# VectorE's share of the softmax exponentials: eight steps a tile against five, four of them over two tiles

## The chip, the cores and the metric

The kernel runs on one core of a Trainium2 chip. The time is the device time of one launch in microseconds; of several runs the median counts. The engines are TensorE (PE in the profile, its weight loads PEld), VectorE (DVE), ScalarE (ACT), GpSimd (POOL) and SyncE (SP), which here only issues DMAs.

## What is computed

Two layers over 2048 tokens of width 448. Each layer is an attention block with 16 heads of 28 columns, followed by a mixing block with two small square matrices and an MLP of width 1792. The part that matters here is attention:

```python
q, k, v = qkv[0], qkv[1], qkv[2]
scores = jnp.einsum("bhqd,bhkd->bhqk", q, k) * (Dh ** -0.5)
p = _softmax(scores, axis=-1)
o = jnp.einsum("bhqk,bhkd->bhqd", p, v)
...
x = x + _A_ref(_layernorm(x, axis=-1), A_wqkv, A_wo)
x = x + _B_ref(_layernorm(x, axis=-1), B_w1, B_w2, B_w3, B_w4)
x = x + _A_ref(_layernorm(x, axis=-1), A_wqkv, A_wo)
x = x + _B_ref(_layernorm(x, axis=-1), B_w1, B_w2, B_w3, B_w4)
```

A layer has 16 heads x 2048 x 2048 exponentials; as tiles of 128 keys by 512 queries that is 1024 tiles, 2048 for both layers. The softmax needs no maximum over the row: every query's scores are shifted by a bound that is written into a spare row of the queries (WSH is a part of it), and a column of ones beside the values gives the sum, by which the result is divided later.

## The kernel before

**Who fixes the order.** The program is not written engine by engine. Small tasks (Python generators) yield operations with an engine, an assumed duration, what they read and write, and a rank; class `Sched` (lines 185 to 539) plays them against assumed durations and puts each engine's instructions in one fixed order; class `Plan` then adds the semaphore waits. On the chip each engine goes through its list in order. Large tables steer this: `RANK` (line 562), the lead at which queries are projected (`Q_LEAD`), which engine does a shared step (`XPAR`, keys 'ez', 'ex', 'ek', 'eo', 'eq': 0 GpSimd, 1 VectorE, 2 whichever is free), and the rates below. Where TensorE would be idle, `keep_pe_busy` puts in filler matmuls (line 2267).

**The stream of score tiles.** Work goes by segments: a chunk of queries, a group of four heads, a range of keys. There are 68 segments with 512 key blocks in all, four tiles (one a head) to a key block. `t_scores` (line 1629) cuts the stream of tiles into units of two or three: even units use PSUM banks 0 to 2, odd units 3 and 4 (and 5 if it is free). The scores come from line 1487; `t_exp` (line 1740) has ScalarE take a whole unit in one instruction (line 1754) into PT. `t_pv` (line 1768) multiplies the exponentials with the values (line 831, four heads side by side) and adds up in bank 7, two key blocks at a time, in the order of the stream.

**Tiles for VectorE.** `ahead_of` (line 1640) picks a tile some key blocks ahead of the stream, so that VectorE has time for it. There are two kinds. A ring tile takes the third bank of an even unit, so that ScalarE's instruction is two tiles wide; it is chosen 6 to 8 blocks ahead (RLO, RHI), if VectorE's planned load over the last 3 us is below XPAR 'dt' and the segment's count is within `R_RATE`. A side tile takes a bank of its own beside the unit, 5 to 7 blocks ahead (DLO, DHI), if the share of fillers over the last 8 us is above XPAR 'ft' and the count is within `D_RATE`. Either needs a y buffer (two in yd, two more in idle parts of vaug at some times) and a PD slot (four, one more in vaug), held until line 831 has used the tile.

**The eight steps.** `d_first` (line 1582) reads the scores from PSUM and writes them as int16 in units of 1/256 of a power of two; `d_chain` (line 1595) turns that into a bf16 value by seven steps over 512 elements: shift out the fraction (line 1611), two factors of a polynomial (1613, 1615, 1617), their product (1619), the sum (1621), and a shift back with the exponent's offset (1624). One of three fb buffers is held from line 1611 to 1621; fb also serves the softmax's division (line 1861) and the tanh form of gelu (line 2034).

Other lines that the prediction names: 1257 (squares of the keys), 1509 (shift of the queries at a new key range).

Of the kernel before, what the change touches and what calls it, by code (L numbers as in the profile page):

```python
# [184 lines left out]
class Sched:  # L185
# [43 lines left out]
    def _advance(self, t):  # L229
        while True:  # L230
# [29 lines left out]
            elif c == "rel":  # L260
# [3 lines left out]
                self.res_t[spec[1]] = max(self.res_t.get(spec[1], 0.0), self.clock)  # L264
            elif c == "reserve":
                if spec[2]:
                    self.reserved.add(spec[1])
                else:
                    self.reserved.discard(spec[1])
            elif c == "wait":  # L270
                if spec[1] not in self.events:
                    self.waiters.setdefault(spec[1], []).append(t)
                    return
            elif c in ("acq", "ready"):
                self.pendq.append(t)
                return
            else:
                self.opq.append(t)
                return
# [270 lines left out]
DST = [0.2, 0.2, 0.336, 0.2, 0.336, 0.336, 0.2]  # L550
DSEG = 1
R_RATE = {(0,): 0, (1,): 0.006, (2,): 0.016, (3,): 0.04, (4,): 0.006, (5,): 0.051, (6,): 0.059, (7,): 0, (8,): 0.06, (9,): 0.048, (10,): 0.024, (11,): 0.15, (12,): 0.066, (13,): 0.022, (14,): 0.022, (15,): 0.192, (16,): 0.233, (17,): 0.075, (18,): 0.115, (19,): 0.273, (20,): 0.093, (21,): 0.233, (22,): 0.355, (23,): 0.29, (24,): 0, (25,): 0.268, (26,): 0.146, (27,): 0.207, (28,): 0.183, (29,): 0.243, (30,): 0.071, (31,): 0.163, (32,): 0.241, (33,): 0.078}
# [9 lines left out]
RANK = {('q', 0, 1): 2.187, ('q', 0, 2): 1.163, ('q', 0, 3): 2.532, ('q', 1, 0): 1.046, ('q', 1, 1): 2.224, ('q', 1, 2): 2.603, ('q', 1, 3): 1.838, ('b', 0, 0): 2.161, ('b', 0, 1): 2.168, ('b', 0, 2): 1.786, ('b', 0, 3): 3, ('b', 0, 4): 1.341, ('b', 1, 0): 2.813, ('b', 1, 1): 2.272, ('b', 1, 2): 2.447, ('b', 1, 3): 2.996, ('b', 1, 4): 1.2, ('a', 0, 0): 1.465, ('a', 0, 1): 1.069, ('a', 0, 2): 2.708, ('a', 0, 3): 1.394, ('a', 0, 4): 2.037, ('a', 1, 0): 2.44, ('a', 1, 1): 2.73, ('a', 1, 2): 1.987, ('a', 1, 3): 2.129, ('a', 1, 4): 2.296, ('k', 0, 1): 2.195, ('k', 0, 2): 2.331, ('k', 0, 3): 1.257, ('k', 1, 0): 2.95, ('k', 1, 1): 2.469, ('k', 1, 2): 2.057, ('k', 1, 3): 1.894, ('k', 1, 4): 1.325, ('c', 0, 0): 2.53, ('c', 0, 1): 1.416, ('c', 0, 2): 2.652, ('c', 0, 3): 2.702, ('c', 0, 4): 2.848, ('c', 1, 0): 1.131, ('c', 1, 1): 1.73, ('c', 1, 2): 1.159, ('c', 1, 3): 1, ('c', 1, 4): 2.718, ('w', 0, 0): 3, ('w', 0, 1): 2.526, ('w', 0, 2): 2.67, ('w', 0, 3): 2.558, ('w', 0, 4): 1.161, ('w', 1, 0): 1.012, ('w', 1, 1): 2.213, ('w', 1, 2): 2.397, ('w', 1, 3): 1.705, ('w', 1, 4): 1.73, ('o', 0, 0): 2.913, ('o', 0, 1): 2.031, ('o', 0, 2): 2.592, ('o', 0, 3): 1.459, ('o', 0, 4): 2.576, ('o', 1, 0): 1.548, ('o', 1, 1): 1.29, ('o', 1, 2): 2.296, ('o', 1, 3): 1, ('o', 1, 4): 2.51, ('v', 0, 1): 1, ('v', 0, 2): 2.093, ('v', 0, 3): 2.749, ('v', 1, 0): 2.464, ('v', 1, 1): 1.304, ('v', 1, 2): 1.601, ('v', 1, 3): 1, ('v', 1, 4): 2.552, ('l', 1, 0): 2.0, ('l', 1, 1): 1.613, ('l', 1, 2): 2.72, ('l', 1, 3): 2.152, ('l', 1, 4): 1.196}  # L562
Q_LEAD = {(0, 1): 7, (0, 2): 102, (0, 3): 50, (1, 0): 86, (1, 1): 54, (1, 2): 9, (1, 3): 71}
# [29 lines left out]
def QLEAD(L, qc):  # L593
    return Q_LEAD[L, qc]

# [5 lines left out]
def build_kernel(nc, A_x, A_wqkv, A_wo, B_x, B_w1, B_w2, B_w3, B_w4, out, n_layers=2):  # L601
# [22 lines left out]
    NPD = 4  # L624
# [1746 lines left out]
```

## Time and profile before

| | |
|---|---|
| median of 3 runs | 1026.12 us (1024.83 to 1026.28) |
| span of the profiled execution, first to last instruction | 1023.9 us |
| busy, share of the span: PE, ACT, DVE, POOL | 95%, 95%, 82%, 21% |
| granted TensorE clock | 1.000 |
| line 1754, first and last start | 15.2 and 968.7 us |

The profile gives the span of the profiled execution; its own device time is not recorded beside it, so the median of the runs stands for it, 2.2 us above the span. In the rows, "us, mean ns" after the bar are the busy time of a group and the mean duration of one instruction, and what follows the second bar is the idle time of that engine before them and what ended it. Rows by stretches give busy microseconds and, in brackets, the number of instructions for each engine in turn, then the granted clock, the DMA engines' share and GB/s.

### The profile page before, as it was taken

The page shows a single profiled execution, that of the slowest core. Times are in us where ns is not written, and L with a number is a line of the kernel's source. Part 1 is how long each engine was busy: PE and PEld are TensorE (multiplying, and loading weights), DVE is VectorE, ACT ScalarE, POOL GpSimd, SP SyncE. Part 2 cuts the span into 40 slices and gives each one's busy share as a digit, 9 for nine tenths or more (in the row PEclk, how much of TensorE's full clock was granted, in tenths as well). Part 3 has the DMA queues.
Part 4 walks back from the last instruction along what each step waited for, and adds up shares of the span by engine and source line. Part 5 has one row for each costly group of instructions (what it writes and reads, how often), then busy time and mean ns, then how long its engine had stood idle before and what let it go on. Part 6 is the DMA issues. An engine that isn't in the chain of part 4 may idle for free.

```text
span 1023.9 us, 36349 instructions
## 1 busy us (share of the span) xinstructions
PE 973.4 (95%) x16102; PEld 404.7 (40%) x16102; DVE 843.5 (82%) x2134; ACT 973.6 (95%) x897; POOL 220.1 (21%) x350
## 2 busy tenths in 40 slices
PE   8999899999999999999999999999999999999998
PEld 4333344334343334344344333333333333444465
DVE  8879999988768778897788888997898888788752
ACT  6899999999999999999999999999999999999942
POOL 4003022143213013350212010112332200331220
PEclk9999999999999999999999999999999999999999
DMA  4534228121203113321133024324311110220000
GB/s 126 130 74 140 59 76 216 34 44 37 33 18 84 43 49 88 51 39 19 36 87 63 22 76 140 112 80 112 74 29 33 32 55 13 55 61 17 13 21 25
DMA packets 98829, 64.43 MB, mean 63 GB/s; under 512 B 70832, under 2 KB 87552, under 8 KB 98672
## 3 DMA queue, kind: packets, MB, share of 16 engines
q1 hardware_dynamic: 94176, 53.11, 21.1%
q0 software_dynamic: 3376, 8.09, 3.0%
q8 instruction: 126, 2.06, 0.9%
q10 hardware_dynamic: 1120, 0.92, 0.3%
q14 instruction: 31, 0.25, 0.1%
HBM read 28.16 MB, written 16.76 MB: 44 GB/s over the span
## 4 chain that ended last, share of the span: by engine, by line
ACT 62%; PE 23%; DVE 12%; DMA 1%; issue 1%; ACTq 0%; SPq 0%; DVEq 0%
ACT PT L1754 55%; PE ps L840 12%; PE ps L1487 5%; PE ps L831 4%; ACT h2T L2220 3%; PE ps L2267 1%; ACT fb L2036 1%; DVE yd L1584 1%; DMA xT<-xnd 1%; DVE fb L1619 1%; DVE fb L1615 1%; DVE PD L1624 1%; DVE ub L1840 1%; DVE vaug L1621 1%; ACT L1754 1%
## 5 line engine op out<-in xcount | busy, mean ns | idle before, releaser
L1754 ACT ACTIVATE PT<-ps 128x1024 bf16<-128x1024 f32 (+1 forms) x791 | 877.8, 1288 | 7.8 <-PE ps L1487 6.6
L1487 PE MATMUL ps<-qT,kT 32*128 32x512 bf16 (+1 forms) x2560 | 310.1, 340 | 23.5 <-ACT PT L1754 17.7
L831 PE MATMUL ps<-PT,vaug 128*32 128x512 bf16 (+1 forms) x2396 | 243.8, 341 | 0.5 <-ACT PT L1754 0.3
L1487 PEld LDWEIGHTS ps<-qT,kT 32*128 32x128 bf16 x2560 | 79.7, 91 | 292.0 <-ACT PT L1754 262.9
L840 PE MATMUL ps<-xT,w 128*32 128x512 bf16 (+3 forms) x2592 | 178.7, 343 | 1.7 <-issue 0.8
L2267 PE MATMUL ps<-ident 128*32 128x256 bf16 x2508 | 123.0, 280 | 2.2 <-POOL ident L930 1.5
L831 PEld LDWEIGHTS ps<-PT,vaug 128*32 128x32 bf16 x2396 | 71.8, 94 | 91.5 <-issue 78.2
L840 PE MATMUL ps<-w,h2T 128*32 128x448 bf16 x1288 | 89.5, 355 | 2.0 <-ACT h2T L2220 2.0
L840 PEld LDWEIGHTS ps<-xT,w 128*32 128x32 bf16 (+1 forms) x2592 | 68.9, 95 | 52.5 <-issue 25.1
L2267 PEld LDWEIGHTS ps<-ident 128*32 128x32 bf16 x2508 | 73.1, 98 | 25.3 <-issue 9.2
L1584 DVE TENSOR_SCALAR yd<-ps 128x512 int16<-128x512 f32 x94 | 64.5, 686 | 21.8 <-PE ps L1487 21.1
L1865 POOL TENSOR_TENSOR otn<-ub,fb 128x512 bf16<-128x512 f32 (+1 forms) x32 | 37.2, 1162 | 189.3 <-DMA fb<-rscr 178.7
L2196 DVE CAST h2T<-ps 128x384 bf16<-128x384 f32 (+1 forms) x84 | 52.0, 619 | 19.7 <-PE ps L840 17.9
L1615 DVE TENSOR_TENSOR fb<-fb 128x512 bf16<-128x512 int16 x112 | 49.0, 438 | 0.7
L840 PEld LDWEIGHTS ps<-w,h2T 128*32 128x32 bf16 x1288 | 34.6, 96 | 31.0 <-issue 12.0
L831 PE MATMUL ps<-PD,vaug 128*32 128x512 bf16 (+1 forms) x146 | 43.9, 342 | 1.2 <-DVE PD L1624 1.0
L840 PE MATMUL ps<-xT,wk_pad 128*32 128x512 bf16 (+1 forms) x512 | 41.2, 369 | 1.8 <-DVE kT L1226 1.2
L2267 PE MATMUL ps<-ident,xn 128*32 128x256 bf16 x896 | 40.8, 274 | 0.6 <-DVE ub L1840 0.6
L840 PE MATMUL ps<-wo_pad,otn 128*32 128x448 bf16 x512 | 36.9, 355 | 3.2 <-DVE x_res L1920 1.7
L1621 DVE TENSOR_TENSOR yd<-yd,fb 128x512 int16<-128x512 int16 x88 | 38.3, 436 | 1.2
L840 PE MATMUL ps<-wv,xT 128*32 128x448 bf16 x480 | 37.7, 356 | 0.6 <-ACT kT L1227 0.2
L840 PE MATMUL ps<-xT,wq_pad 128*32 128x512 bf16 x448 | 36.8, 382 | 1.4 <-DVE kT L1226 0.8
(238 smaller groups left out, 1318.0 us busy)
## 6 DMA issues: line engine op xcount, KB each, us to landing
uscr<-ub SPq DMA_DIRECT2D x28, 256.0 KB
ub<-uscr SPq DMA_DIRECT2D x28, 256.0 KB
fb<-rscr SPq DMA_DIRECT2D x96, 64.0 KB, 2.1
xnd<-xn SPq DMA_DIRECT2D x28, 128.0 KB, 3.1
x_res<-in_A_x_dram POOLq DMA_DIRECT2D x16, 224.0 KB, 3.3
xd<-x_res SPq DMA_DIRECT2D x16, 224.0 KB, 2.3
x_res<-xd SPq DMA_DIRECT2D x16, 224.0 KB, 4.1
out_dram<-obf SPq DMA_DIRECT2D x16, 112.0 KB, 1.8
```

Source lines behind the costliest of these rows:

```text
L831: return lambda e: e.matmul(out=out, lhsT=lhsT, rhs=rhs, start=start, stop=stop, **kw)
L840: r.append(e.matmul(out=out[c:c + w, :], lhsT=lhsT[:, c:c + w], rhs=rhs, start=start, stop=stop, tile_position=(0, c)))
L1487: yield op("pe", (0.005 + NW * 0.00042) / nc_, lambda e, i=i, kc=kc, j=j, g=g, a=a, NW=NW, bank=bank: e.matmul(out=ps[:, bank, i * NW:(i + ...
L1584: yield op("dve", c_ps(512), lambda e: e.tensor_scalar(out=y.bitcast(I16)[:, 0:512], in0=ps[:, bi(bank), :], scalar1=SCALE * L2E * FS, sca ...
L1615: yield op("dve", D_[2], lambda e: e.tensor_tensor(out=z, in0=qa, in1=qa, op=ALU.mult), reads=fk, writes=fk, urge=urge, two=True)
L1619: yield op("dve", D_[4], lambda e: e.tensor_tensor(out=z, in0=z, in1=w, op=ALU.mult), reads=yk + fk, writes=fk, urge=urge, two=True)
L1621: yield op("dve", D_[5], lambda e: e.tensor_tensor(out=ya, in0=ya, in1=z, op=ALU.add), reads=yk + fk, writes=yk, urge=urge, two=True)
L1754: yield op("act", 0.0635 + n * w * 0.000833, lambda e, bk=bk, s0=s0, n=n, w=w: e.activation(out=PT[:, s0:s0 + n, 0:w], in_=ps[:, bk[0]:bk[ ...
L1865: yield both(("eo", L, ch), 0.2 + NW * 0.0021, 0.07 + NW * 0.00104, lambda e: e.tensor_tensor(out=otn[:, g, 0:NW], in0=u, in1=rb[:, 0:NW], ...
L2196: ev = op("dve", c_ps(m * NW), lambda e, hr=hr, pv=pv: e.tensor_copy(out=hr, in_=pv), reads=[("ps", bi(b))], writes=hk, touch=[b])
L2220: yield op("act", c_act(len(fr_) * NW), lambda e, v=v: e.activation(out=v, in_=v, func=ACT.Gelu_apprx_tanh), reads=allk, writes=allk, tab= ...
L2267: return [e.matmul(out=ps[32 * c:32 * c + 32, bi(b), 0:256].rearrange("p (a n) -> p a n", n=128), lhsT=xn[:, 0, D:D + 32] if live else ide ...
```

## The change

**The arithmetic.** The shift of the scores (WSH) now holds 127 ln 2 more, ScalarE's exponential subtracts it again through its bias (XB in place of ln 2), and `d_first` writes int16 in units of 1/128, clamped at 0. That is a bf16 number's own bit pattern with a straight line between powers of two. The chain masks the 7-bit fraction f, forms EG f + EB, multiplies by f and adds the product to the pattern: a quadratic in place of the polynomial of before. There is no shift and no last step; the sum is written in place in the PD slot.

**Two tiles at once.** The steps behind `d_first` run over a pair of tiles that lie side by side, 1024 elements. A slot is now a pair (PD has eight tiles, four slots; vaug lends two more); yd is gone. `take` opens a pair with the first tile and shuts it with the second; if the stream comes within DFL = 4 key blocks of the first tile of an open pair, it is shut with one. The chain is spawned when the pair is shut and all its first steps are planned. It holds two fb buffers, of which the first is freed after the product, and at most two chains run at a time ('dc0', 'dc1'). The assumed durations are DST: 0.2, 0.2, 0.336, 0.336 for one tile, 0.336, 0.336, 0.602, 0.602 for two.

**The order.** A new planner command, `prio`, lets tasks wait at rank 2 and take their rank from RANK when their inputs are there. All tables have new values. Of those the prediction uses the following; a cap is rate x 4 x key blocks, summed over the segments, and 'dt' is listed for each group of four segments:

| | before | after |
|---|---|---|
| caps from R_RATE, D_RATE (tiles) | 244, 515 | 313, 513 |
| 'dt' | .742 .628 .931 .713 .834 .726 .895 .621 .514 .772 .784 .935 .934 .521 .861 .55 .703 | 1.2 .978 .922 1.003 .92 .704 1.2 .349 .957 .869 .632 1.12 .871 .92 .954 1.0 .88 |
| mean of 'dt' | .745 | .911 |
| layer 0 and 1, 'ex' on VectorE outright | 6 and 4 of 16 | 10 and 7 of 16 |
| PE_NORM in use (last head group of a chunk normalised through TensorE) | none | chunks 0 and 3 of layer 1 |

```diff
-    WSH = 60.0 / SCALE
+    WSH = (60.0 + 127.0 * math.log(2.0)) / SCALE
...
-    FS = 256.0
+    FS = 128.0
+    XB = math.log(0.99835146) - 127.0 * math.log(2.0)
...
-    EA, EB, EG = 21.0427, 88.0467, -0.244205
+    EG, EB = 0.33575143 / 128.0, -0.34288473
...
-    NPD = 4
+    NPD = 8
...
-        yd = sb("yd", [128, 2, 512], I32)
...
+        def d_first(blk, bank, ring=None):
+            y, yk = ibuf(blk)
+            yield op("dve", c_ps(512), lambda e: e.tensor_scalar(out=y.bitcast(I16), in0=ps[:, bi(bank), :], scalar1=SCALE * L2E * FS, scalar2=0.0, op0=ALU.mult, op1=ALU.max),
...
+            pr = pair_of[blk]
+            pr["got"] += 1
+            if pr["shut"] and pr["got"] == len(pr["blks"]):
+                yield ("spawn", d_chain(pr), XPAR["dp", blk[0] // 4])
...
-            yield op("dve", D_[0], lambda e: e.tensor_scalar(out=qu, in0=yu, scalar1=8, scalar2=32768, op0=ALU.logical_shift_left, op1=ALU.bitwise_xor),
-            yield op("dve", D_[1], lambda e: e.tensor_scalar(out=w, in0=qa, scalar1=EA / 65536.0, scalar2=EB, op0=ALU.mult, op1=ALU.add),
-            yield op("dve", D_[2], lambda e: e.tensor_tensor(out=z, in0=qa, in1=qa, op=ALU.mult),
-            yield op("dve", D_[3], lambda e: e.tensor_scalar(out=z, in0=z, scalar1=1.0 / 65536.0 ** 2, scalar2=EG, op0=ALU.mult, op1=ALU.add),
-            yield op("dve", D_[4], lambda e: e.tensor_tensor(out=z, in0=z, in1=w, op=ALU.mult),
-            yield op("dve", D_[5], lambda e: e.tensor_tensor(out=ya, in0=ya, in1=z, op=ALU.add),
-            yield op("dve", D_[6], lambda e: e.tensor_scalar(out=pdt.bitcast(U16), in0=yu, scalar1=32768, scalar2=1, op0=ALU.bitwise_xor, op1=ALU.logical_shift_right),
+            tok = yield ("acq", ["dc0", "dc1"], yk)
+            f1 = yield ("acq", xtra("f") + FB)
+            f2 = yield ("acq", xtra("f") + FB)
+            (q, fk), (v, wk) = fbuf(f1), fbuf(f2)
+            fu, w = q.bitcast(U16)[:, 0:512 * n], v.bitcast(BF16)[:, 0:512 * n]
+            yield op("dve", D_[0], lambda e: e.tensor_scalar(out=fu, in0=yu, scalar1=127, scalar2=None, op0=ALU.bitwise_and),
+            yield op("dve", D_[1], lambda e: e.tensor_scalar(out=w, in0=fu, scalar1=EG, scalar2=EB, op0=ALU.mult, op1=ALU.add),
+            yield op("dve", D_[2], lambda e: e.tensor_tensor(out=w, in0=w, in1=fu, op=ALU.mult),
+            yield op("dve", D_[3], lambda e: e.tensor_tensor(out=ya, in0=ya, in1=w, op=ALU.add),
...
+                if open_pair:
+                    si1, kb1, _ = min(open_pair[0]["blks"])
+                    if si1 < si0 or kb1 + (len(seg_kb[si0]) if si1 > si0 else 0) <= kb0 + DFL:
+                        yield from shut()
...
-            SC.spawn(t_kv(1, c), RANK["k", 1, c])
+            SC.spawn(t_kv(1, c), 2)
```

137 lines of the change are left out of this document (80 added, 57 removed).

## The prediction, on record before the result

> **What bounds the kernel now.** I read the page first (span, engine shares, the chain that ended last), then the busy time by stretches of the span, then the ScalarE groups by shape, then the VectorE groups, then a piece of VectorE's timeline.
>
> ```profile
> span 1023.9 us, 36349 instructions
> ...
> PE 973.4 (95%) x16102; PEld 404.7 (40%) x16102; DVE 843.5 (82%) x2134; ACT 973.6 (95%) x897; POOL 220.1 (21%) x350
> ...
> ACT 62%; PE 23%; DVE 12%; DMA 1%; issue 1%; ACTq 0%; SPq 0%; DVEq 0%
> ...
> L1754 ACT ACTIVATE PT<-ps 128x1024 bf16<-128x1024 f32 (+1 forms) x791 | 877.8, 1288 | 7.8 <-PE ps L1487 6.6
> ...
> L1487 PEld LDWEIGHTS ps<-qT,kT 32*128 32x128 bf16 x2560 | 79.7, 91 | 292.0 <-ACT PT L1754 262.9
> ```
>
> ScalarE's exponentials (line 1754) are 877.8 us of the span and most of the chain. They wait for scores for 6.6 us only, while the loading of weights for the score matmuls stands still 262.9 us for ScalarE. The stretches say the same (columns: PE, PEld, DVE, ACT, POOL busy):
>
> ```profile
> 0.00:22.00 22.00, 18.93 (x325) 10.04 (x325) 18.42 (x67) 15.32 (x22) 9.02 (x21) 1.00 0.47 140
> 22.00:971.00 949.00, 905.31 (x14623) 363.17 (x14623) 805.44 (x2028) 938.75 (x848) 204.70 (x316) 1.00 0.26 63
> 971.00:1024.00 53.00, 49.19 (x1161) 31.48 (x1154) 19.67 (x41) 19.55 (x29) 6.35 (x15) 1.00 0.08 25
> ```
>
> Between a head of 22 us and a tail of 53 us lies a stage of 949 us in which ScalarE works 938.75 (98.9%) and VectorE 805.44 (84.9%). So in this stage the time is the number of exponentials that ScalarE must take, and VectorE's spare time decides how many it needn't.
>
> **What one tile costs ScalarE.** A tile is 128x512 scores.
>
> ```profile
> L1754 ACT ACTIVATE PT<-ps 128x1536 bf16<-128x1536 f32 x332 | 503.2, 1540 | 5.9 <-PE ps L1487 5.3
> L1754 ACT ACTIVATE PT<-ps 128x1024 bf16<-128x1024 f32 x459 | 482.3, 1106 | 1.8 <-PE ps L1487 1.3
> ...
> L1584 DVE TENSOR_SCALAR yd<-ps 128x512 int16<-128x512 f32 x94 | 64.5, 686 | 21.8 <-PE ps L1487 21.1
> ...
> L1584 DVE TENSOR_SCALAR vaug<-ps 128x512 int16<-128x512 f32 x40 | 27.3, 685 | 4.6 <-PE ps L1487 4.4
> ```
>
> 332 x 3 + 459 x 2 = 1914 tiles on ScalarE, 94 + 40 = 134 on VectorE, 2048 in all. A "ring" tile (it takes the third bank of a unit) turns a three-tile instruction into a two-tile one: 1540 - 1106 = 434 ns. A "side" tile leaves the stream altogether: 877.8 / 1914 = 459 ns on average. These are the two ends; I take 0.45 us for a tile that moves.
>
> **What one tile costs VectorE, before.** Instructions overlap at their ends, so I price by distance between starts, in a stretch where nothing is waited for:
>
> ```profile
> 109.42 0.68 DVE L1584 TENSOR_SCALAR yd<-ps 128x512 int16<-128x512 f32 x1
> 110.02 0.28 DVE L1624 TENSOR_SCALAR PD<-vaug 128x512 uint16<-128x512 uint16 x1
> 110.22 0.68 DVE L1584 TENSOR_SCALAR yd<-ps 128x512 int16<-128x512 f32 x1
> 110.82 0.48 DVE L1611 TENSOR_SCALAR fb<-yd 128x512 uint16<-128x512 uint16 x2
> 111.22 0.49 DVE L1613 TENSOR_SCALAR yd<-fb 128x512 bf16<-128x512 int16 x2
> 111.62 0.42 DVE L1615 TENSOR_TENSOR fb<-fb 128x512 bf16<-128x512 int16 x1
> 111.96 0.35 DVE L1509 TENSOR_SCALAR qT<-qT,db 128x512 bf16<-128x512 bf16 x1
> ...
> 115.07 0.43 DVE L1621 TENSOR_TENSOR yd<-yd,fb 128x512 int16<-128x512 int16 x1
> 115.53 0.29 DVE L1624 TENSOR_SCALAR vaug<-yd 128x512 uint16<-128x512 uint16 x1
> ```
>
> The first step out of PSUM takes 0.60, a step with one source (lines 1611, 1613, 1617, 1624) 0.20, a step with two (1615, 1619, 1621) 0.34. Eight steps: 0.60 + 4 x 0.20 + 3 x 0.34 = 2.42 us a tile, 324 us for 134 tiles. All else that VectorE does in the stage is 805.4 - 324 = 481 us.
>
> **After.** The first step stays (0.60). Removed are the shift, the square and the last shift; left are a mask and a multiply-add (one source) and a product and a sum (two sources), over 1024 elements where two tiles share a slot. No such width is in this trace. For the two-source step the width can be read off:
>
> ```profile
> L1257 DVE TENSOR_TENSOR obf<-kT 128x512 bf16<-128x512 bf16 x8 | 3.4, 423 | 0.2
> ...
> L1257 DVE TENSOR_TENSOR obf<-kT 128x256 bf16<-128x256 bf16 x2 | 0.6, 306 | 0.1
> ```
>
> 256 elements more cost 117 ns, so 512 more about 0.25: 0.34 + 0.25 = 0.59. For the one-source step nothing is fixed but the ends, 0.20 (width free) and 0.40 (all in proportion); I take 0.33, nearer to proportion. A pair then costs 2 x 0.33 + 2 x 0.59 = 1.84, or 0.60 + 0.92 = 1.52 a tile (ends 1.14 and 1.68). A tile that finds no partner goes alone: 0.60 + 2 x 0.20 + 2 x 0.34 = 1.68. How many pair up: a ring tile is chosen 6 to 8 key blocks ahead, and its slot is shut when the stream is within 4 (DFL), so it stays open for two blocks at least; 949 us over 512 key blocks is 1.85 us each, so 3.7 us, against some 4.6 us between tiles on average. As tiles come in runs (rates from 0 to over 1), I put 70% in pairs (ends 40% and 95%): **1.57 us a tile** (1.62 to 1.53), where it was 2.42.
>
> **How many tiles VectorE takes.** At an occupancy p of a stage of T = 949 - 0.45 (N - 134), p T = 485 + 1.57 N; the 485 is 481 and some 4 us for residual adds and squares that the new table gives to VectorE outright instead of GpSimd. With p as now (0.849) N = 190; with 0.88, 205; with 0.95, 237. The planner's gates speak for more than now: the VectorE load above which it gives no ring tile ('dt', mean of 17 values) goes from 0.745 to 0.911, and the ring tiles that R_RATE allows (rate x 4 x key blocks, over 68 segments) from 244 to 313; the side tiles' cap stays (515, 513). Against more: the stretches with spare PE time are nearly full on VectorE already.
>
> ```profile
> 96.00:256.00 160.00, 147.96 (x2432) 62.65 (x2428) 148.86 (x403) 158.13 (x142) 38.26 (x50) 1.00 0.30 79
> 256.00:640.00 384.00, 371.23 (x6073) 146.58 (x6065) 307.94 (x734) 383.11 (x344) 78.53 (x138) 1.00 0.24 57
> 640.00:768.00 128.00, 120.62 (x1861) 47.75 (x1862) 117.44 (x312) 127.54 (x116) 30.23 (x36) 1.00 0.32 81
> ```
>
> VectorE stands at 93%, 80% and 92%. I take p = 0.88: **N = 205, 71 tiles more, 71 x 0.45 = 32 us off ScalarE.**
>
> **What is given back.** The middle stretch has little PE time to spare; the filler matmuls (line 2267), which run where PE would be idle, show it:
>
> ```profile
> 96.00:256.00 160.00, 60.97 (x1280) 36.69 (x1280) 1.00 0.30 79
> 256.00:640.00 384.00, 24.42 (x592) 16.34 (x592) 1.00 0.24 57
> 640.00:768.00 128.00, 40.55 (x803) 22.89 (x807) 1.00 0.32 81
> ...
> 96.00:256.00 160.00, 24.02 (x35) 1.00 0.30 79
> 256.00:640.00 384.00, 27.43 (x40) 1.00 0.24 57
> 640.00:768.00 128.00, 17.15 (x25) 1.00 0.32 81
> ```
>
> (First three lines: filler; last three: line 1584, one instruction a tile.) 24.4 us of filler in 384 us, against 61 in 160. The middle's share of the 32 us is 384 / 949, 13 us; PE work there doesn't shrink, so I charge 5 of them (ends 0 and 13). [...]
>
> **Edits at nothing.** The offset in WSH and in the exponent's bias changes constants of instructions that run anyway. The freed buffer yd pays for four more PD tiles. The chain needs two of the three fb buffers, for four steps instead of one for six; normalisation and the tanh form of gelu use them too, and would be late if they found none. The new order (RANK, Q_LEAD, when the weights' memset on GpSimd and the SP queue's transposing loads are due) I price at 0: the stage's whole ScalarE idle time is 10 us, the tail is a chain of 53 us with PE busy for 49; ends -5 and +5. Two more head groups are normalised through PE (PE_NORM), a few small matmuls and VectorE steps in place of SP's small DMAs: under 1 us each of VectorE time, hidden.
>
> **Sum.** Stage 949 - 32 + 5 = 922; span 22 + 922 + 53 = 997. The span lies 2.2 us under the median of the runs (1026.12 - 1023.9), which I carry over: **999 us**.
>
> **Rivals.**
> 1. *PE bounds the middle and the ends; only the slack stretches gain.* In 96:256 and 640:768 (60 tiles, VectorE 92.5% full over 288 us) the new price gives 0.925 (288 - 0.45 (N - 60)) = 121 + 1.57 N, N = 86, 26 tiles more, 11.5 us: 1014.5. For it: PE busy 371 of 384 in the middle. Against: the weight loads' waits. Chance 0.20 (1008 to 1019).
> 2. *VectorE is filled to 95%.* N = 237, 103 x 0.45 = 46, less 5: 985. For it: the gates, and the two stretches above 92% already. Against: load so high delays PSUM evacuations that PE waits for. Chance 0.17 (977 to 990).
> 3. *It doesn't do what it says: no more tiles move.* Only 134 of the 759 that the caps allowed were taken, so slots, PE idle gates or key projections may limit, and these stay. VectorE then merely idles more. 1026, by order 1020 to 1031. Chance 0.10.
> 4. *Late pairs (slower).* A first tile waits for its partner, then for four wide steps; the value matmul (line 831) that needs it stands in PE's order, and behind it the next scores, which ScalarE needs. Room: 4 key blocks, 7.4 us. A chain now takes 5 to 6 us from its first step (109.42 or 110.22) to its last (115.53); four of seven steps, wide, some 4. Queued behind two other pairs (2 x 1.84) it just fits; behind three it is 2 us late, of which the unit already scored hides one ScalarE instruction (1.1): some 0.7 us lost. 72 pairs and 61 singles are 133 chains; if 60% of them lose 0.5 us, 40 us: 1039. From 27 / 0.5 = 54 late chains of 133 on, the change is a loss.
>
> ```profile
> L831 PE MATMUL ps<-PD,vaug 128*32 128x512 bf16 (+1 forms) x146 | 43.9, 342 | 1.2 <-DVE PD L1624 1.0
> ```
>
>    Against it: value matmuls wait 1.2 us for VectorE's tiles now. Chance 0.08.
>
> **How the numbers follow.** Forecast 0.45 (990 to 1008), rivals 0.20, 0.17, 0.10, 0.08. Range 981 to 1020: the forecast, the first rival, two thirds of the second, an edge of the third: 0.8. Some 0.2% (2 us) is what a measurement can tell here. Faster: 0.45 + 0.20 + 0.17 + 0.04 = 0.86; the same: 0.04 (part of rival 3); slower: 0.02 + 0.08 = 0.10.
>
> **What would show it.** Line 1584's successor should count near 205, ScalarE's tiles near 1843 with fewer three-tile instructions; 1024-wide steps near 0.33 and 0.59 between starts; VectorE's occupancy of the stage near 0.88; ScalarE's idle time in the stage up from 10 to some 15 us, in the middle. A count near 134 is rival 3; value matmuls that wait tens of us for PD are rival 4. The prediction is wrong above all if N is: each 10 tiles are 4.5 us.

## The result, and the profile after

The changed kernel takes 1012.24 us (median of 4 runs, 1010.55 to 1018.02), the kernel before 1026.2 us (1024.83 to 1027.44) beside it: ratio 0.9874, 95% interval 0.9844 to 0.9904. It is 14 us faster where 27 were forecast, and inside the range of 981 to 1020. The profiled run has a span of 1009.2 us and took 1011.01.

Three parts of the page of the kernel after: the span, the engines' shares, and under the chain that ended last the groups of the exponentials (now line 1788) and of the weight loads for the scores (now line 1494).

```profile
span 1009.2 us, 35163 instructions
...
PE 964.2 (96%) x15692; PEld 396.1 (39%) x15692; DVE 838.4 (83%) x1799; ACT 946.0 (94%) x897; POOL 198.4 (20%) x325
...
ACT 62%; PE 32%; DVE 4%; DMA 1%; issue 1%; POOL 1%; ACTq 0%; DVEq 0%
...
L1788 ACT ACTIVATE PT<-ps 128x1024 bf16<-128x1024 f32 (+1 forms) x789 | 849.9, 1256 | 9.1 <-PE ps L1494 8.1
...
L1494 PEld LDWEIGHTS ps<-qT,kT 32*128 32x128 bf16 x2560 | 79.9, 91 | 285.8 <-ACT PT L1788 258.1
```

The exponentials fell from 877.8 to 849.9 us, by 27.9; the span only by 14.7. In the chain VectorE's share went from 12% to 4%, TensorE's from 23% to 32%. The stretches (columns: PE, PEld, DVE, ACT, POOL busy) say where the rest went:

```profile
0.00:22.00 22.00, 18.85 (x325) 10.01 (x325) 17.89 (x67) 15.14 (x22) 8.83 (x21) 1.00 0.46 140
22.00:955.00 933.00, 894.40 (x14201) 353.73 (x14201) 796.54 (x1684) 910.85 (x846) 180.10 (x285) 1.00 0.25 64
955.00:1009.20 54.20, 50.94 (x1181) 32.32 (x1169) 23.92 (x49) 20.02 (x31) 9.45 (x20) 1.00 0.09 27
```

The stage went from 949 to 933 us, by 16.0. In it ScalarE works 27.9 us less (938.75 to 910.85) and idles 933 - 910.85 = 22.15 us where it idled 10.25: 11.9 more. The tail grew by 1.3 us (52.9 to 54.2). Of ScalarE's 11.9 us of new idle time the forecast had charged 5; so of the 12 us by which the profiled run missed it, 6.9 are idle time. The tiles, by the groups of ScalarE and of VectorE (first step, now line 1590, then the four wide steps):

```profile
L1788 ACT ACTIVATE PT<-ps 128x1024 bf16<-128x1024 f32 x518 | 531.2, 1105 | 3.5 <-PE ps L1494 3.0
L1788 ACT ACTIVATE PT<-ps 128x1536 bf16<-128x1536 f32 x271 | 414.9, 1543 | 5.6 <-PE ps L1494 5.1
```

```profile
L1590 DVE TENSOR_SCALAR PD<-ps 128x512 int16<-128x512 f32 x160 | 109.6, 687 | 26.1 <-PE ps L1494 24.8
...
L1631 DVE TENSOR_TENSOR PD<-PD,fb 128x1024 int16<-128x1024 int16 x55 | 38.1, 694 | 0.7
L1628 DVE TENSOR_TENSOR fb<-fb 128x1024 bf16<-128x1024 bf16 x53 | 36.4, 686 | 0.8
...
L1590 DVE TENSOR_SCALAR vaug<-ps 128x512 int16<-128x512 f32 x39 | 26.4, 686 | 2.6 <-PE ps L1494 2.2
L1626 DVE TENSOR_SCALAR fb<-fb 128x1024 bf16<-128x1024 uint16 x53 | 22.5, 424 | 1.1
L1624 DVE TENSOR_SCALAR fb<-PD 128x1024 uint16<-128x1024 uint16 x50 | 21.4, 430 | 0.3
```

518 x 2 + 271 x 3 = 1849 tiles on ScalarE, 160 + 39 = 199 on VectorE; 71 pairs (line 1631 over 1024 columns, all its tiles counted), so 142 of 199 tiles (71%) go in pairs. Most of the idle time stands at one place. The waits of ScalarE, and its timeline there:

```profile
ACT PT L1788 <- PE ps L1494: 8.1, 11, 2.7
...
ACT hT L2056 <- DVE hT L2043: 5.3, 1, 5.3
ACT h2T L2258 <- DVE h2T L2234: 5.2, 1, 5.2
```

```profile
467.12 2.46 ACT L1788 ACTIVATE PT<-ps 128x1024 bf16<-128x1024 f32 x2
469.60 1.28 ACT L2056 ACT_TABLE_LOAD   x1
476.21 1.06 ACT L2056 ACTIVATE hT<-hT 112x1024 bf16<-112x1024 bf16 x1 [5.33 <-DVE hT L2043]
482.49 6.18 ACT L2258 ACTIVATE h2T<-h2T 128x7168 bf16<-128x7168 bf16 x1 [5.22 <-DVE h2T L2234]
488.69 1.28 ACT L1788 ACT_TABLE_LOAD   x1
489.98 1.94 ACT L1788 ACTIVATE PT<-ps 128x1024 bf16<-128x1024 f32 x2
```

At 469.60 ScalarE has done the last exponential of layer 0; it changes its table, waits 5.33 us, does a gelu, waits 5.22, does another, and starts layer 1 at 489.98. The two waits are 10.5 of the 11.9 us. TensorE meanwhile:

```profile
469.86 1.99 PE L843 MATMUL ps<-xT,w 128*32 128x256 bf16 x40
472.21 1.48 PE L843 MATMUL ps<-xT,w 128*32 128x512 bf16 x32 [0.36 <-DVE h2T L2234]
474.06 1.48 PE L843 MATMUL ps<-xT,w 128*32 128x512 bf16 x32 [0.36 <-DVE h2T L2234]
475.90 5.74 PE L843 MATMUL ps<-xT,w 128*32 128x512 bf16 x96 [0.36 <-DVE h2T L2234]
481.58 1.88 PE L843 MATMUL ps<-w,hT 112*32 112x448 bf16 x32
483.40 4.13 PE L843 MATMUL ps<-xT,wq_pad 128*32 128x512 bf16 x64
...
488.99 0.60 PE L1494 MATMUL ps<-qT,kT 32*128 32x512 bf16 x5
```

It is busy for 18.4 of these 20.4 us, with layer 0's last mixing and MLP matmuls and then layer 1's first queries (483.40); the first scores of layer 1 (line 1494) come at 488.99. In the kernel before, no wait of this size stands at the boundary: its gelus follow at once there (from 496.33 to 506.06), and ScalarE is busy for 79.9 of the 80 us from 440 to 520.

**Runs and the clock.** The changed kernel was run three times over, 15 runs from 1009.41 to 1018.07 us. They follow the mean granted clock of TensorE of each run: 1.000 gives 1009.41 and 1009.75, 0.998 gives 1010.55 to 1011.01, 0.995 gives 1013.46 and 1013.75, 0.990 gives 1018.02 and 1018.07. A straight line, 1009.2 us + 0.84 us for each thousandth of clock, fits them all within 1.0 us (0.5 in the root mean square). The kernel before has a clock of 1.000 in 39 of the 54 runs beside the experiments, with a median of 1025.5 us. So at a full clock the change is worth 16.3 us, and the dips of the clock take up to 9 of them. Below, "at full clock" is the mean of a kernel's runs, each brought to 1.000 by this slope: an estimate that holds for dips like the changed kernel's; differences under 1 us are not read.

### The profile page after: what moved, and what is told of

It is laid out like the page before. It is cut to its first block, busy times and chain, and to the rows that moved or that the text cites. A ratio compares the mean times of both kernels' runs of the same rounds, so it can differ in the third digit from the quotient of the medians.

```text
span 1009.2 us, 35163 instructions
## 1 busy us (share of the span) xinstructions
PE 964.2 (96%) x15692; PEld 396.1 (39%) x15692; DVE 838.4 (83%) x1799; ACT 946.0 (94%) x897; POOL 198.4 (20%) x325
## 4 chain that ended last, share of the span: by engine, by line
ACT 62%; PE 32%; DVE 4%; DMA 1%; issue 1%; POOL 1%; ACTq 0%; DVEq 0%
ACT PT L1788 55%; PE ps L843 17%; PE ps L1494 8%; PE ps L834 5%; ACT h2T L2258 3%; PE ps L2305 1%; ACT fb L2074 1%; ACT L1788 1%; ACT hT L2056 1%; DVE fb L1628 0%; DMA PT<-in_A_wqkv_dram 0%; DVE h2T L2234 0%; DMA xT<-xn 0%; ACT L2258 0%; ACT L2056 0%
## 5 line engine op out<-in xcount | busy, mean ns | idle before, releaser
L1788 ACT ACTIVATE PT<-ps 128x1024 bf16<-128x1024 f32 (+1 forms) x789 | 849.9, 1256 | 9.1 <-PE ps L1494 8.1
L1494 PE MATMUL ps<-qT,kT 32*128 32x512 bf16 (+1 forms) x2560 | 310.4, 340 | 19.7 <-ACT PT L1788 14.7
L1494 PEld LDWEIGHTS ps<-qT,kT 32*128 32x128 bf16 x2560 | 79.9, 91 | 285.8 <-ACT PT L1788 258.1
L843 PE MATMUL ps<-xT,w 128*32 128x512 bf16 (+4 forms) x2592 | 172.9, 343 | 2.6 <-DVE h2T L2234 1.7
L1590 DVE TENSOR_SCALAR PD<-ps 128x512 int16<-128x512 f32 x160 | 109.6, 687 | 26.1 <-PE ps L1494 24.8
L2305 PE MATMUL ps<-ident 128*32 128x256 bf16 x1980 | 96.4, 281 | 1.6 <-POOL ident L933 1.5
L2305 PEld LDWEIGHTS ps<-ident 128*32 128x32 bf16 x1980 | 57.2, 99 | 19.8 <-issue 6.9
L834 PE MATMUL ps<-PD,vaug 128*32 128x512 bf16 (+1 forms) x208 | 58.3, 335 | 1.1 <-DVE PD L1631 1.1
L1631 DVE TENSOR_TENSOR PD<-PD,fb 128x1024 int16<-128x1024 int16 (+1 forms) x95 | 56.9, 600 | 1.3
L1628 DVE TENSOR_TENSOR fb<-fb 128x1024 bf16<-128x1024 bf16 (+1 forms) x89 | 51.4, 577 | 1.5
L2305 PE MATMUL ps<-ident,xn 128*32 128x256 bf16 x984 | 44.6, 275 | 1.2 <-issue 0.9
L843 PE MATMUL ps<-w,hT 112*32 112x448 bf16 x512 | 35.2, 355 | 3.6 <-ACT hT L2056 2.7
```

The source lines that it names most:

```text
L834: return lambda e: e.matmul(out=out, lhsT=lhsT, rhs=rhs, start=start, stop=stop, **kw)
L843: r.append(e.matmul(out=out[c:c + w, :], lhsT=lhsT[:, c:c + w], rhs=rhs, start=start, stop=stop, tile_position=(0, c)))
L1494: yield op("pe", (0.005 + NW * 0.00042) / nc_, lambda e, i=i, kc=kc, j=j, g=g, a=a, NW=NW, bank=bank: e.matmul(out=ps[:, bank, i * NW:(i + ...
L1590: yield op("dve", c_ps(512), lambda e: e.tensor_scalar(out=y.bitcast(I16), in0=ps[:, bi(bank), :], scalar1=SCALE * L2E * FS, scalar2=0.0, ...
L1628: yield op("dve", D_[2], lambda e: e.tensor_tensor(out=w, in0=w, in1=fu, op=ALU.mult), reads=fk + wk, writes=wk, urge=urge, two=True)
L1631: yield op("dve", D_[3], lambda e: e.tensor_tensor(out=ya, in0=ya, in1=w, op=ALU.add), reads=yk + wk, writes=yk, urge=urge, two=True)
```

## The experiments

Kernels with the changed kernel's "own order" keep the emitted instructions of every engine, their sequence and their waits, but for the edit; in e2, e3 and e4 a memset on GpSimd at the start also sets the columns left out to 1. Two theories at first. **A**: TensorE is full up to the layer boundary and sets when layer 1's scores come. **B**: ScalarE bounds the stage; the stall at the boundary merely stands behind its stream.

**e1: the changed kernel again.** No edit.

> The changed kernel itself once more, as the yardstick for the three beside it. All theories: 0.987 of the kernel before (range of the first comparison 0.984 to 0.990), some 13 us faster; ScalarE idle 10 to 11 us between about 469 and 483 us, while the last MLP group of layer 0 waits for its matmuls. If the single TensorE clock dips that the first runs showed (mean clock 0.990 to 0.998 with 1016 to 1009 us) belong to this kernel, they come again and the spread stays near 7 us; if they were chance, the mean clock is 1.000 and the runs agree within 3 us.

Measured: 1010.76 us (1009.41 to 1015.75), ratio 0.9866 (0.9843 to 0.9889); waits of 5.3 and 5.2 us as before; clocks 0.993, 0.998, 0.992, 1.000, 1.000. The dips come again; the kernel before beside it has 0.998 in three of nine runs and nothing lower. So they belong to this kernel.

**e2 and e3: exponentials 16 columns narrower in one layer.**

```
-  e.activation(out=PT[:, s0:s0 + n, 0:w], in_=ps[:, bk[0]:bk[0] + n, 0:w], ...)
+  e.activation(out=PT[:, s0:s0 + n, 0:w - cut], in_=ps[:, bk[0]:bk[0] + n, 0:w - cut], ...)   # cut 16 in layer 0 (e2) or 1 (e3)
```

> The changed kernel in its own order, with ScalarE's exponentials of layer 0 over 496 instead of 512 columns of each tile (the last 16 columns of those tiles are left at 1). 16 columns are 16 x 434/512 = 13.6 ns a tile, some 920 tiles, 12.5 us of ScalarE work less ahead of the boundary between the layers. Theory A (before the boundary TensorE is full and sets when layer 1's first scores exist; ScalarE only runs out of tiles earlier): 0 to 4 us faster than the changed kernel, ScalarE's idle time between 440 and 490 us up from 11 to about 20. Rival B (ScalarE bounds the stage throughout, and the boundary's matmuls stand queued behind its tiles in TensorE's order): 11 to 13 us faster, idle time at the boundary unchanged at 11.

> The same cut of 16 columns in layer 1's tiles only (left at 1): some 12.5 us of ScalarE work less behind the boundary. Theory A and rival B both: 9 to 12.5 us faster than the changed kernel, since layer 1 has TensorE time to spare; a theory in which the whole stage hangs on TensorE or VectorE: under 4.

Measured: e2 1007.88 us (ratio 0.9821, 0.98 to 0.9842), at full clock 1004.4, 4.8 less than the changed kernel; e3 1008.52 (0.9835, 0.9822 to 0.9849), at full clock 1004.0, 5.2 less (as measured, 2.9 and 2.2 less than e1 beside them). ScalarE's waits at the boundary are 5.6 and 5.2 us in e2. Both theories miss: in e2 the idle time didn't grow to 20 (A), and neither kernel gained 9 to 13 (B in e2, both in e3). e3's third reading, under 4, is just missed too. ScalarE's groups in e2, by shape:

```profile
L1791 ACT ACTIVATE PT<-ps 128x1024 bf16<-128x1024 f32 x274 | 279.0, 1105 | 2.9 <-PE ps L1494 2.2
L1791 ACT ACTIVATE PT<-ps 128x992 bf16<-128x992 f32 x244 | 238.9, 1028 | 2.4 <-PE ps L1494 1.4
L1791 ACT ACTIVATE PT<-ps 128x1488 bf16<-128x1488 f32 x145 | 207.0, 1446 | 6.7 <-PE ps L1494 5.8
L1791 ACT ACTIVATE PT<-ps 128x1536 bf16<-128x1536 f32 x126 | 193.8, 1540 | 2.5 <-PE ps L1494 2.4
```

The 145 instructions over three tiles can give 145 x 41 ns = 5.9 us, the 244 over two 244 x 27 = 6.6. From start to start (taken from the trace's single records) the median goes from 904 to 877 ns over two tiles and from 1330 to 1290 over three, as it should. But in layer 0 the mean over two tiles is 937 ns in the changed kernel and 942 after the cut: steps that had waited for scores now wait longer, and steps that hadn't now do. The mean over three goes from 1339 to 1301, 5.3 us over the layer. So only the three-tile instructions paid. Such waits are nearly invisible in the columns above: an instruction lasts 1105 ns in the mean and its successor starts after 904, so a wait of up to about 0.2 us leaves ScalarE busy throughout. Taken from start to start, 106 steps over two tiles come more than 25 ns late in the changed kernel, by 16.4 us together, of which 5.4 show as idle time; in the kernel before 98 steps lose 14.4 us, of which 3.9 show.

**e4: the same cut in the kernel before.**

> The kernel before, in its own order, with ScalarE's exponentials of layer 0 16 columns narrower (left at 1): some 950 tiles x 13.6 ns = 13 us of ScalarE work less ahead of the boundary. Theory A (the boundary was not far behind ScalarE there: TensorE busy 371 of 384 us in the middle, ScalarE waits 0.3 us at the boundary): part of it, 4 to 9 us faster than the kernel before, and new idle time of ScalarE between 470 and 490. Rival B: 12 to 13 us faster, no new idle time.

Measured: 1020.93 us (0.9954, 0.9941 to 0.9966), at a full clock in all runs, 4.6 less than 1025.5; no new idle time at the boundary (79.9 of 80 us busy from 440 to 520). A's number with B's picture. The point for the prediction: in the kernel before, too, 13 us of ScalarE work were worth under 5.

That calls for another theory. **C**: TensorE paces the two-tile units and the boundary, ScalarE the three-tile ones.

**e5 and e6: value matmuls a quarter narrower in one layer.**

```
-  mm(ps[32 * j:32 * j + 32, PVBANK, 0:NW], vaug[...], buf[:, s, i * NW:(i + 1) * NW], done == 0, ...)
+  mm(ps[32 * j:32 * j + 32, PVBANK, 0:WP if done else NW], vaug[...], buf[:, s, i * NW:i * NW + (WP if done else NW)], done == 0, ...)   # WP = 3/4 NW
```

> The changed kernel in its own order, with the value matmuls of layer 0 a quarter narrower (all but the first of each segment add to 384 of 512 or 192 of 256 queries only, so a quarter of the queries lack most of their sum): some 990 tiles x 128 columns, by the kernel's own price of 0.104 ns a column and tile 13 us of TensorE work less ahead of the boundary between the layers. Theory C (new, after narrower exponentials gave 3 to 5 of 12.5 us: TensorE paces the units of two tiles and the stretch up to the boundary, ScalarE only the units of three): 6 to 12 us faster than the changed kernel (1009.5 at an unthrottled clock, 1011 in the middle of its runs), the idle time of ScalarE at the boundary well under its 10.5 us. Rival B (ScalarE bounds): within 2 us of it.

> The same quarter of the value matmuls left out in layer 1 only (13 us of TensorE work less behind the boundary). Theory C: 4 to 10 us faster than the changed kernel, and fewer or no dips of the TensorE clock near 700 us if these come from TensorE's load. Rival B: within 2 us, but for what the dips cost (1 to 5 us).

Measured: e5 1013.43 us (0.9874, 0.9847 to 0.99), e6 1015.8 (0.9872, 0.9826 to 0.9918): no faster, but at lower clocks (0.988 to 0.998, and 0.985 to 0.998). The run of each at 0.998 took 1009.11 and 1006.66, where the changed kernel at 0.998 takes 1010.55 to 1011.01: 1.7 and 4.1 us less. By the slope it is 2.8 and 4.9. The boundary's waits stay at 5.3 and 5.2. C's 6 to 12 in e5 is a miss; in e6 4.9 lies in its 4 to 10, but only at full clock, and the dips became more, not fewer: down to 0.988 and 0.985 with less for TensorE to do, where the changed kernel's lowest is 0.990.

**e7: no fillers.** All filler matmuls between 30 and 940 us of the plan are left out, their waits kept.

> The changed kernel in its own order without the filler matmuls that its plan puts into TensorE's idle time between 30 and 940 us. Theory C with fillers that stand in the way of scores: 3 to 10 us faster, no dips near 700 us. Theory C with fillers only in true gaps: within 2 us. A third outcome is open: if the clock or the matmuls' pace falls without them, 10 us and more slower.

Measured: 1041.01 us (1.0148, 1.0132 to 1.0163), clock 0.916 to 0.921. The third outcome: with the fillers the clock is 0.990 to 1.000, and leaving them out costs 30 us.

**e8: the new steps on one tile at a time, in the order of before.** The square, one multiply-add and the last shift are dropped; 134 tiles stay on VectorE.

> The kernel before, in its own order and with its own 134 VectorE tiles, each in the new arithmetic (offset in the shift, mask, multiply-add, product, sum) on one tile at a time: 134 x (2.42 - 1.68) = 99 us of VectorE work less, nothing moved off ScalarE. All theories that I hold: within 3 us of the kernel before, VectorE's busy time down by 80 to 100 us. A theory in which the gain comes from VectorE being late (late PD tiles, late evacuations): 5 to 15 us faster.

Measured: 1022.73 us (0.9969, 0.9957 to 0.998), 2.8 less than 1025.5 and 3.2 less than the runs beside it. VectorE's busy time fell from 843.5 to 744.8 us:

```profile
PE 970.9 (95%) x16099; PEld 404.0 (40%) x16102; DVE 744.8 (73%) x1732; ACT 972.3 (95%) x897; POOL 214.5 (21%) x350
```

About as expected (3 us at most): 99 us off VectorE are worth some 3 here. A cheaper chain by itself is worth next to nothing; it must move tiles.

**e9 and e10: less MLP work for TensorE ahead of the boundary.**

```
# e9: two of four blocks of the inner sum left out for layer 0's last group
+  None if L == 0 and tiles[0] == 7 and fc in (1, 2) else (mm4 if NW > 200 else mm)(ps[...], w3[:, fc, ...], ...)
# e10: 128 queries fewer in all of layer 0
-  ps[:, bi(b), k * NW:(k + 1) * NW], ... xv(xt)[:, fc, 0:NW]
+  ps[:, bi(b), k * NW:k * NW + WN], ... xv(xt)[:, fc, 0:WN]
```

> The changed kernel in its own order; the last MLP group of layer 0 (tiles 7 to 10) takes half of the inner sum of its first matmuls (two of four blocks of 128 left out). Its matmuls are what TensorE works on while ScalarE has no scores at the boundary: ten pieces of 0.96 us each from 469.9 to 481.6 us would take about 0.5. Theory C (TensorE's queue of MLP matmuls sets the boundary): ScalarE's idle time there falls from 10.5 to 5 to 7 us, layer 1's first exponential starts 4 to 5 us earlier, and the kernel is 3 to 5 us faster than the changed one (1009.5 at an unthrottled clock). Rival E (the chain from the second key norm over the transposing load to the queries sets it): idle time unchanged, within 1.5 us. Rival G (what the boundary loses is taken back later, because the rest waits for something else): idle time falls, but the kernel stays within 1.5 us.

> The changed kernel in its own order, with the first MLP matmuls of all of layer 0 128 queries narrower (a quarter to a third of the queries left out there): some 10 us of TensorE work less ahead of the boundary, out of the pieces behind which scores stand. Theory C: 3 to 7 us faster than the changed kernel, two-tile units in layer 0 nearer to their bare 903 ns than 939. Rival B: within 2 us.

Measured: e9 1013.29 us (0.9868, 0.9852 to 0.9884) at clocks of 0.992 to 0.995, at full clock 1007.5, 1.7 less. Its waits at the boundary:

```profile
ACT hT L2072 <- DVE hT L2059: 3.9, 1, 3.9
ACT h2T L2274 <- DVE h2T L2250: 3.7, 1, 3.7
```

7.6 us instead of 10.5, where C said 5 to 7: the queue of MLP matmuls does set part of the stall (E is out). Of the 2.9 us some 1.7 arrive at the end, which is under C's 3 to 5 and hardly over G's 1.5. e10 1013.01 us (0.9867, 0.9851 to 0.9883), at full clock 1007.4, 1.8 less: C's 3 to 7 is missed, and so is its other sign: in layer 0 the steps over two tiles stay at 937 ns. TensorE's work as such isn't the bound either.

**e11: fillers against the dips.** After each fourth value matmul from 676 to 696 us of the plan, one filler that adds zeros.

> The changed kernel in its own order, with one filler (four matmuls of zeros added to the value sum) behind each fourth value matmul between 676 and 696 us. If the dips of the clock near 696 us come from too little TensorE activity there, they are gone, and the five runs lie within 2 us of each other at 1009 to 1011. If they come from too much, or from the chip, the spread of 6 us and clocks of 0.990 to 0.998 stay.

Measured: 1013.32 us (0.9869, 0.9853 to 0.9884), clocks 0.995 to 0.997. A miss as put: the dip near 697 us lasts 3.4 us in this profile, as in the changed kernel's first one (10.2 us in e1's), and others came at 149 and 654.

**e12: the wide steps as halves.**

```
-  e.tensor_scalar(out=fu, in0=yu, scalar1=127, ...)
+  [e.tensor_scalar(out=fu[:, c], in0=yu[:, c], scalar1=127, ...) for c in hs]      # hs: 512 columns each; so in all four steps
```

> The changed kernel in its own order, with each wide step over two tiles as two steps over one: 71 x 4 instructions more, by the prediction's prices 71 x 2 x (2 x 0.20 + 2 x 0.34 - 0.33 - 0.59) / 2 = 11 to 23 us more of VectorE time, nothing else changed. If VectorE has room (85% busy): within 1.5 us. If its lateness is part of the loss (the five steps alone took 3 us off the kernel before): 2 to 8 us slower.

Measured: 1020.71 us (0.9932, 0.9905 to 0.9958), 1014.95 in the run with a clock of 1.000: some 5 us slower than the changed kernel.

```profile
PE 976.2 (95%) x15692; PEld 398.6 (39%) x15692; DVE 855.9 (84%) x2083; ACT 949.6 (93%) x897; POOL 195.6 (19%) x325
```

VectorE has 855.9 instead of 838.4 us, 17.5 more at 84% busy, and 5 of them come out at the end. VectorE's spare time is not free either in the changed kernel; that this is so because more tiles hang on it fits, but isn't shown.

**e13 and e14: each half of the change alone.** Theory **H**: the new steps need the new order, and the order belongs to the gain. Rival **I**: the order costs what the steps gain.

```
# e13: the changed kernel, the six tables of before        # e14: the kernel before, the six tables of after
R_RATE, RANK, Q_LEAD, D_RATE, PE_NORM, XPAR
```

Only the tables change sides: the `prio` command stays in e13 and is missing in e14. In both, the plan is made anew.

> The changed kernel (five steps, pairs, its code for the order) with the tables of the kernel before (rates of ring and side tiles, ranks, leads, normalisation): the new arithmetic alone, the plan made anew by the kernel's own planner. By that planner's own forecast 167 VectorE tiles and a stall of ScalarE of 14 us near 244 us; against the chip its forecasts stand 7 to 8 us low, so 1030 to 1037 us. Theory H (the steps' gain needs the new order; the order is part of the gain, not a loss by itself): slower than the changed kernel by 20 to 27 us and no faster than the kernel before. Rival I (the order costs what the steps gain, the stall at the boundary is its fault alone): 1005 us or less.

> The kernel before with the tables of the changed one: the new order alone, old arithmetic, the plan made anew. By the planner 135 VectorE tiles and 1034 + 7 = 1038 to 1044 us. Theory H: slower than the kernel before by 12 to 18 us. Rival I: slower too, but with ScalarE idle some 10 us at the layer boundary as in the changed kernel; under H the idle time stands elsewhere (the planner has it near 551 us).

Measured: e13 1027.71 us (1.0012, 1.0002 to 1.0023), e14 1046.24 (1.0184, 1.0156 to 1.0212; at full clock 1038.8). H holds, though e13 is some 2 us better than its numbers and e14's raw time a little worse. At full clock the steps with the old tables cost 2 us, the new tables with the old steps 13, and both together gain 16. e13 has 136 + 31 = 167 tiles on VectorE and no stall at the boundary, where the gelus follow at once, but one of 13.4 us elsewhere (e13's timeline, then its first wait; after it the first waits of e14):

```profile
498.26 3.72 ACT L1788 ACTIVATE PT<-ps 128x1536 bf16<-128x1536 f32 x3
501.99 1.28 ACT L2056 ACT_TABLE_LOAD   x1
503.28 1.06 ACT L2056 ACTIVATE hT<-hT 112x1024 bf16<-112x1024 bf16 x1
504.25 6.16 ACT L2258 ACTIVATE h2T<-h2T 128x7168 bf16<-128x7168 bf16 x1
```

```profile
ACT PT L1788 <- PE ps L834: 13.4, 1, 13.4
```

```profile
ACT PT L1754 <- PE ps L1487: 23.2, 20, 8.9
```

e14 loses 23 us in waits of exponentials for scores, and none at the boundary. So the stall of the changed kernel comes neither of the steps alone nor of the tables alone: it is where this pair of them falls short.

**e15: a plan with a shorter stall.** Layer 1's first queries wait for a third buffer of transposed tiles, and the tables were searched anew.

```
+            if (L, qc) == (1, 0):
+                yield ("wait", ("third",))
```

> The changed kernel with the first queries of layer 1 waiting for a third buffer of transposed tiles instead of one of two, and tables searched anew for it: the planner has 192 VectorE tiles (199 in the changed kernel), ScalarE's idle time at the boundary at some 8 us of its scale instead of 15. If the stall is a loss that can be had back: 1003 to 1007 us at an unthrottled clock. If the stall is the price of tiles moved in a TensorE that is full up to the boundary: within 2 us of the changed kernel's 1009.5.

Measured: 1012.71 us (0.9874, 0.9834 to 0.9915), 1010.32 in the run at a full clock. The boundary's wait is 5.5 us instead of 10.5, VectorE has 155 + 37 = 192 tiles instead of 199: 7 x 0.43 = 3.0 us more for ScalarE against 5.0 us less of stall, and no gain. Here the stall behaves like the price of the tiles. One plan, made anew in more than the stall, suggests it; a better one is not excluded.

**e16: e11's fillers from 140 to 160 and 636 to 716 us.**

> The changed kernel in its own order with one filler behind each fourth value matmul from 140 to 160 and from 636 to 716 us (e11 had them from 676 to 696, and the profiled run kept one window at half clock at 698.7 and one at 654.3). If too little TensorE activity sets the dips: mean clock 0.998 to 1.000 in all runs, spread under 2 us, 1009 to 1012 us. If not: clocks of 0.990 to 0.997 as before.

Measured: 1008.71 us (1008.29 to 1010.81), ratio 0.9831 (0.9811 to 0.9852), clocks 0.998, 1.000, 1.000, 1.000. As expected. It beats the kernel before clearly. Its ratio lies under the changed kernel's three (0.9874, 0.9866, 0.9891), which weren't taken beside it; at full clock it is 0.5 us under 1009.2, so what it gains is what the dips cost. The stretch of the dip in the changed kernel, and then in e16 (the last columns are the granted clock, the DMA share, GB/s):

```profile
690.00:693.00 3.00, 3.00 (x30) 1.55 (x28) 2.97 (x7) 3.00 (x5) 0.00 (x0) 1.00 0.00 0
693.00:696.00 3.00, 2.71 (x24) 1.59 (x21) 2.53 (x7) 3.00 (x4) 0.48 (x1) 1.00 0.52 135
696.00:700.00 4.00, 4.00 (x33) 0.93 (x33) 4.00 (x9) 3.61 (x4) 0.79 (x1) 0.57 0.76 161
```

```profile
690.00:693.00 3.00, 3.00 (x35) 1.78 (x34) 2.97 (x8) 3.00 (x4) 0.00 (x0) 1.00 0.00 0
693.00:696.00 3.00, 3.00 (x30) 1.59 (x28) 2.40 (x7) 3.00 (x4) 0.26 (x1) 1.00 0.33 108
696.00:700.00 4.00, 3.76 (x49) 1.29 (x46) 4.00 (x9) 4.00 (x5) 1.01 (x1) 1.00 0.72 152
```

24 matmuls in 3 us, and the next 3.4 us go at half the clock; 30, and they don't. The count is no rule, though (see the last section).

**e17 and e18: the changed kernel beside still more fillers** (140 to 200, 420 to 450, 590 to 760, 915 to 945 us).

> The changed kernel beside e18 on one chip. Clocks of 0.990 to 1.000 and 1009.4 to 1018 us as in its nine runs before, by 0.84 us for each thousandth of clock.

> The changed kernel in its own order with e16's fillers (one behind each fourth value matmul) over 140 to 200, 420 to 450, 590 to 760 and 915 to 945 us of the plan. If too little TensorE activity sets all dips: clock 1.000 but for one window at the start, 1008 to 1010 us, 1 to 5 us under the changed kernel's median. If so many fillers begin to stand in front of scores: 1011 us and more at a full clock.

Measured: e17 1014.45 us (0.9891, 0.9869 to 0.9912) at clocks of 0.990 to 0.998; e18 1016.72 (0.9917, 0.9898 to 0.9937), clock 1.000 in four of six runs, the profiled one among them. In these four the clock is held, and the second branch came: 1014.39 to 1016.96 us at a full clock, 5 to 8 over the changed kernel's 1009.2. That the 625 matmuls more (16317 against 15692) stand in front of other work is the likely reason; no run shows it apart.

## Why the prediction was wrong, point by point

- **The count of tiles: right; VectorE's price: right in part by luck.** N = 199 where 205 were forecast, 71% in pairs (70%). VectorE's occupancy of the stage is 796.54 / 933 = 0.854 (0.88). With the prediction's own 485 us for all else a tile costs (796.5 - 485) / 199 = 1.57 us, the forecast number. But no run shows the 485. Counted from the trace's single records in the stage, each instruction up to the next start or to its own end, a tile costs 2.76 us before and 1.76 after, and all else 434 and 445 us. The prediction took its prices where steps of different tiles alternate; a step that needs the one ahead starts later (0.46 us after line 1621 in the prediction's own rows, priced at 0.34). The tile came out too cheap and the rest too dear, and the two cancel. ScalarE lost 27.9 us instead of 32: six tiles fewer, and 27.9 / 65 = 0.43 us a tile instead of 0.45.
- **"What is given back" failed**: 5 us charged, 11.9 measured. It was placed in the middle by the share of the stretch 256 to 640, and the place is right, but 10.5 of it is one stall at the layer boundary, in which TensorE works through the MLP of layer 0 and layer 1's queries (e9: less of that MLP, a shorter stall). The fillers were the wrong gauge: there were 24.4 us of them in the stretch, spread over it, and that says nothing of a queue of 18 us that this plan puts between the last score of one layer and the first of the next.
- **"The new order I price at 0" failed with it.** e13 and e14 show that the order isn't neutral: 18 us lie between the changed kernel with its own tables and with the old ones (1009.2 and 1027.5 at full clock), and 13 between the old kernel's two. The order can't be priced as a term by itself.
- **"So in this stage the time is the number of exponentials that ScalarE must take" is too strong.** 98.9% busy said so, and e4 shows 4.6 us for 13 us of ScalarE work in the kernel before; e2 and e3 5 for 12.5. Every engine that was relieved or loaded with the order held moved the end by a part only: value matmuls 2 to 5 us of 13, VectorE 5 of 17.5 (loaded) and 2.8 of 99 (relieved). The gain of the change, 16 of 27.9, is more than such cuts give; that the new plan makes the difference fits e13 and e14, but wasn't shown apart. What paces the two-tile steps is not settled: of the 106 late steps of the changed kernel most have a piece of projection or MLP matmuls right ahead of their scores, which is read from the trace and wasn't shown by an edit (narrower pieces in e10 left the steps at 937 ns).
- **"Two more head groups are normalised through PE ... hidden" left out the clock.** Of VectorE's time it may be so. But in all three profiles of the changed kernel the clock dips at 696 to 697 us (0.50 from 696.2 to 699.5 in the first, 0.81 from 690 to 700 in e1's), right behind the small matmuls of the first of the two groups (690.0 to 695.9 in the first profile). That these cause the dip isn't shown: no run left them out alone, e15 has them at the same place without a dip there, and other dips stand at 430 and 652 us. What the dips cost is: the median lies 1.2 us over the profiled run, whose clock was 0.998, and a single run lost up to 9.
- **The sum.** 999 forecast; +4.1 (exponentials: 27.9 for 32), +6.9 (idle time), +1.3 (tail) = 1011.3, the profiled run's 1011.0; +1.2 to the median, whose runs had lower clocks.
- **Rivals.** Rival 1 gave 1014.5 and named TensorE in the middle: nearer in time, but its count (160 tiles) is wrong by 39. Rivals 2 and 3 fall with N = 199. Rival 4 falls: value matmuls wait 1.1 us for VectorE's tiles. The weight loads' waits, held against rival 1, don't rule such a loss out: they wait 258.1 us for ScalarE here too, and a queue of TensorE still stops ScalarE for 10.5 us.

## What to carry to other kernels

A busy share of 99% says that an engine has no long gaps; whether its time is the kernel's time is seen from the distance between starts (the median step, where nothing is waited for, against the mean step), since ends that overlap hide short waits (here a two-tile exponential is busy for 1105 ns in the mean, and where nothing is waited for the next starts after 904). When work is moved off such an engine, ask of each serial passage, as between two layers, what must run there before the engine has work again, and charge that passage whole, not by its share of the span. Where a plan is tuned to its prices, new prices with the old plan, or the new plan with old prices, can each be slower than what was there: forecast the pair.

## What the runs showed of the hardware

- TensorE's granted clock is 1.00 throughout the profile of the kernel before; in the changed kernel's first one it is 1.00 but for one piece of 3.4 us at 0.50, from 696 us. Without fillers it is 0.92 in the mean and the kernel 31.8 us slower (1041.0 against 1009.2); with narrower value matmuls it falls as low as 0.985, where the changed kernel had 0.990; with some 160 matmuls more, from 140 to 160 and from 636 to 716 us of the plan, it is 1.000 in three of four runs. One such piece costs some 1.4 us, an estimate from the 15 runs (0.84 us for each thousandth; a piece is 1.7 thousandths of the span).
- TensorE was busy 2.71 of 3.00 us by its columns just ahead of the dip at 696 us, so it was hardly idle there. What sets off a dip stays open: from 693 to 696 us the changed kernel had 24 matmuls in its first profile and 29 in e17's and lost the clock behind both; e16 kept it with 30, but so did e15 with 22:

```profile
693.00:696.00 3.00, 2.75 (x22) 1.07 (x17) 2.97 (x8) 3.00 (x5) 0.16 (x1) 1.00 0.45 128
696.00:700.00 4.00, 3.71 (x62) 1.89 (x66) 3.70 (x8) 3.33 (x4) 1.27 (x1) 1.00 0.92 212
```

- In a pair that nothing else interleaves, the dependent wide steps on VectorE don't overlap: they last 0.43, 0.43 and 0.69 us and start 0.46, 0.46 and 0.73 us apart, where 0.33, 0.33 and 0.59 were forecast. Where a step that doesn't need them came next, the median from start to start was 0.34 us behind the mask (line 1624, 0.42 long) and 0.61 behind the product and the sum (lines 1628 and 1631, 0.68 long), near the forecast; behind the multiply-add (line 1626, 0.42 long) it was 0.44.

```profile
301.05 0.43 DVE L1624 TENSOR_SCALAR fb<-PD 128x1024 uint16<-128x1024 uint16 x1
301.51 0.43 DVE L1626 TENSOR_SCALAR fb<-fb 128x1024 bf16<-128x1024 uint16 x1
301.97 0.69 DVE L1628 TENSOR_TENSOR fb<-fb 128x1024 bf16<-128x1024 bf16 x1
302.70 0.69 DVE L1631 TENSOR_TENSOR PD<-PD,fb 128x1024 int16<-128x1024 int16 x1
```
